# GpSimd put into written order as well, with a pair's values, turns, low parts and reciprocals written at earlier places

## The chip, the cores and the metric

One core of a Trainium2 chip runs the whole program. The time is device microseconds of that core, from runs of the same program; a profiled execution has a time of its own beside its span. The engines that matter are TensorE (PE: matmuls and transposes, into PSUM), VectorE (DVE), ScalarE (ACT), GpSimd (POOL) and SyncE (SP, which issues most transfers).

## The reference

```python
# 1. attention, 8 batches x 8 heads, 576 tokens, head size 64
scores = q @ k.T / 8                       # block mask: block(i) >= block(j), blocks of 64
attn   = exp(scores - max) ; attn /= sum + 1e-9
x      = (attn @ v) with heads side by side          # 8 x 576 x 512
# 2. token mixing of rank 32, then an MLP 512 -> 2048 -> 512
u = x + (x.T @ U @ V).T
y = u + relu(u @ w_ch1) @ w_ch2
# 3. gate: depthwise causal convolution over 5 tokens
out = (sigmoid(conv(y)) * (y @ w_val)) @ w_out
```

## The kernel before

**Tiles.** The 4608 tokens are cut into nine groups of 512. The MLP of a group runs in 16 steps of 128 hidden columns. A step's `emit_h1` is 12 matmuls into one PSUM bank (names `h`, three products for each of four pieces, since the float32 numbers are split into a high and a low part); ACT then makes the high part `hh` (L1167) and DVE the low part `hl` (L1168). `emit_o` is 12 matmuls that add the step before into four banks `acc`. Attention goes by pairs of heads: 32 pairs p, two heads a and b each. The stretch that the change touches is the one in which the MLP of groups 1 to 6 runs together with the attention of pairs 10 to 31.

**Order.** The MLP's matmuls are the ground, and after each half of `emit_h1` and of `emit_o` there is a gap, in which `gap` lets pieces of attention in. A pair takes `PERIOD` = 16 gaps. `events(p)` is the written table: each line gives the gap at which a piece is let in, whether it is one that PE takes part in (at most one of those in a gap), and the piece. Within an offset the pieces come in the order of the lines. Three pairs are under way at a time: p (scores, maxima, exponentials), q = p - 1 (values, normalising, transposing) and r = p - 2 (token mixing). PE's instructions always stand as the program writes them; from group 1 to group 6 those of DVE and ACT do as well (`manual_schedule`), while the order of POOL's is left to the scheduler. An offset only settles a place in each engine's queue: an engine starts no instruction before the one ahead of it.

**The pieces that matter here.**
- `scores(p, 0)` and `scores(p, 2)`: two halves of the score matmuls (L416), each half four PSUM banks; ACT copies every bank out (L421).
- `maxima(n)`, `max_c(n)`: a head's row maxima on DVE (L614, L633, L635, L636; then L647 to L657 and the transpose L660). `soften_sub(n)`: five subtractions on DVE (L667). `soften_exp(n)`: two exponentials on ACT (L683), then `emit_sum_a`, four additions on POOL (L690, L692). `emit_sum_b`: two reductions on DVE (L699).
- `values(q)`: the products with v (L733, L743), two banks `pPV`, copied out by ACT (L745).
- `pv_norm(q)`: three DVE instructions (L715, the reciprocal L716, the transpose L718) and one POOL multiplication of 128x576 (L719), which finishes the tile `xt`.
- `turn_all(q)`: transposes of `xt` on PE (L822, L824), two banks `pT`, and their high parts on ACT; `turn_lo(q)`: their low parts on DVE (L101, `x<-pT,x`).
- `g_product`, `g_sum`, `g_split`, `h_begin`, `h_end`: token mixing of pair r (names `pG`, `pH`, `ul`).

All of `h`, `pS`, `pPV`, `pT`, `pG` and `pH` share four PSUM banks in this stretch (`ps_p`); which bank a tile gets is settled when the program is built, and its first matmul waits for whoever read that bank last.

Of the kernel before, what the change touches and what calls it, by code (L numbers as in the profile page):

```python
# [22 lines left out]
def attn_moe_gate_kernel(ctx: ExitStack, tc: tile.TileContext, q, k, v, U, V, w1, w2, wval, convw, wout, out):  # L23
    nc = tc.nc
    B, H, S, D = q.shape
# [8 lines left out]
    NP = H // 2  # L34
# [54 lines left out]
    def f32(ap):  # L89
        return ap if ap.dtype == F32 else ap.bitcast(F32)  # L90
# [3 lines left out]
    def hi_act(o, i):  # L94
        act.copy(o, i)  # L95
# [4 lines left out]
    def lo(eng, o, i, h):  # L100
        eng.tensor_tensor(o, i, f32(h), op=ALU.subtract)  # L101
# [142 lines left out]
    def rot(tag, bufs=2, dtype=F32, n=S):  # L244
        return rot_p.tile([P, n], dtype, tag=tag, bufs=bufs, name=tag)
# [425 lines left out]
    def ev(n, j, a=0):  # L671
        return est[n][half_of[j]][:, soff[j] + a:soff[j] + wid[j]]
# [22 lines left out]
    def emit_sum_b(n):  # L695
        m = sums[n]
        r = tiny_p.tile([P, NB32], F32, tag="rs", bufs=3, name="rs")
        for o, t in ((slice(0, P // BL), ev(n, 0)[:, 0:P]), (slice(P // BL, NB32), m)):
            vec.tensor_reduce(r[:, o], t.rearrange("p (b a) -> p b a", a=BL), axis=AX.X, op=ALU.add, apply_transpose=True)  # L699
        sums[n] = r  # L700
# [12 lines left out]
    def pv_norm(pn, xt, f):  # L713
        r = tiny_p.tile([P, NB32], F32, tag="r0", name="r0")
        vec.tensor_scalar(r, f, 1e-9, None, op0=ALU.add)  # L715
        vec.reciprocal(r, r)  # L716
        rb = rot("t")
        vec.transpose(rb.rearrange("p (j a) -> p j a", a=32), r.rearrange("p (j o) -> p j o", o=1).to_broadcast([P, NB32, 32]))  # L718
        pool.tensor_tensor(xt, xt, rb, op=ALU.mult)  # L719
# [34 lines left out]
    normed = {}  # L754
# [57 lines left out]
    def turn_all(pn):  # L812
        xt = xts[pn]
        full = S // P
        if not xfix:
            xfix.append(rot("x", 1, F32R, NTT * 2 * P).rearrange("p (i c m) -> p i c m", c=2, m=P))
            pool.memset(f32(xfix[0][tok[-1][1]:, NTT - 1]), 0.0)
        x = xfix[0]
        gst[pn] = x
        ps = [ps_p.tile([P, 512], F32, tag="a", name="pT") for _ in range(2)]  # L820
        for i in range(full):
            pe.transpose(ps[0][:, i * P:(i + 1) * P], xt[:, i * P:(i + 1) * P], ident)  # L822
        t0, n = tok[full]
        pe.transpose(ps[1][:n, 0:P], xt[:, t0:t0 + n], ident)  # L824
        pairs = [(x[:, 0:full], ps[0][:, 0:full * P].rearrange("p (i m) -> p i m", m=P)), (x[:n, full:full + 1], ps[1][:n, 0:P].rearrange("p (i m) -> p i m", m=P))]
        for t, pv in pairs:
            hi_act(t[:, :, 0, :], pv)
        open_t[pn] = pairs

    def turn_lo(pn):  # L830
        for t, pv in open_t.pop(pn):
            lo(vec, t[:, :, 1, :], pv, t[:, :, 0, :])

    def g_product(pn):
        x = gst[pn].rearrange("p i c m -> p i (c m)")
        ps = ps_p.tile([P, 512], F32, tag="a", name="pG")
        for i in range(NTT):
            pe.matmul(ps[:, 0:2 * P], ust1[:, i, :], x[:, i, :], start=(i == 0), stop=(i == NTT - 1))
        open_t[pn] = ps

    def g_sum(pn):
        ps = open_t.pop(pn)
        g32 = rot("t")[:, 0:P]
        act.copy(g32, ps[:, 0:P])
        vec.tensor_tensor(g32, ps[:, P:2 * P], g32, op=ALU.add)
        open_t[pn] = g32

    def g_split(pn):
        g32 = open_t.pop(pn)
        g = rot("g", 4, F32R, P)  # L850
        hi_act(g, g32)
        lo(vec, g[2 * R:3 * R], g32[2 * R:3 * R], g[2 * R:3 * R])
        gst[pn] = g
# [68 lines left out]
    def soften_sub(n):  # L922
        emit_sub(n, 0)
        emit_sub(n, 1)

    def soften_exp(n):
        emit_exp(n)
        emit_sum_a(n)

    def max_c(n):  # L930
        for _ in emit_max_c(n):
            pass

    def maxima(n):
        emit_max_a(n)
        emit_max_b(n)

    def h_begin(pn, i):
        if i >= len(mix_pieces(pn // NP)):
            return  # L940
        if held(pn, i):
            later.append((pn, i))
        else:
            h_product(pn, i)

    def h_end(pn, i):
        if (pn, i) in open_h:
            h_sum(pn, i)
        if i and pn % NP == NP - 1:
            ready.add(pn // NP)  # L950
# [5 lines left out]
    def values(p):  # L956
        emit_pv(p, 0)
        emit_pv(p, 1)

    def events(p):  # L960

        a, b = 2 * p, 2 * p + 1
        new, q, r = a < NH, p - 1, p - 2
        first_ = p == PAIR0
        if new:
            yield 0, 1, lambda: scores(p, 0)
            yield 0, 0, lambda: (load_v(a), load_v(b))
        if first_:
            yield 2, 1, lambda: turn_all(r)
            yield 3, 0, lambda: turn_lo(r)  # L970
            yield 4, 1, lambda: g_product(r)
        else:
            yield 2, 1, lambda: g_product(r)
            yield 3, 0, lambda: g_sum(r)
            if q < B * NP:
                yield 3, 0, lambda: soften_exp(2 * q + 1)
            yield 4, 0, lambda: g_split(r)
        if new:
            yield 4, 1, lambda: scores(p, 2)
            yield 5, 0, lambda: (emit_corners(a), emit_corners(b), prep_t(p + 1))  # L980
        if first_:
            yield 6, 0, lambda: g_sum(r)
            yield 7, 0, lambda: g_split(r)
            yield 8, 1, lambda: h_begin(r, 0)
        else:
            yield 6, 1, lambda: h_begin(r, 0)
            if q < B * NP:
                yield 7, 0, lambda: emit_sum_b(2 * q + 1)
            yield 7, 0, lambda: h_end(r, 0)
            yield 7, 1, lambda: h_begin(r, 1)  # L990
            yield 8, 0, lambda: h_end(r, 1)
        if new:
            yield 8, 0, lambda: maxima(a)
        if q < B * NP:
            yield 9, 1, lambda: values(q)
        if new:
            yield 9, 0, lambda: max_c(a)
            yield 10, 0, lambda: soften_sub(a)
        if first_:
            yield 10, 0, lambda: h_end(r, 0)  # L1000
            yield 10, 1, lambda: h_begin(r, 1)
            yield 11, 0, lambda: h_end(r, 1)
        if q < B * NP:
            yield 12, 0, lambda: pv_norm(q, *normed.pop(q))
        if new:
            yield 12, 0, lambda: maxima(b)
            yield 12, 0, lambda: soften_exp(a)
        if q < B * NP:
            yield 14, 1, lambda: turn_all(q)
        if new:  # L1010
            yield 15, 0, lambda: max_c(b)
        if q < B * NP:
            yield 16, 0, lambda: turn_lo(q)
        if new:
            yield 16, 0, lambda: (emit_sum_b(a), soften_sub(b))

    def pair_tick(p):
        for off, pe_step, what in events(p):
# [361 lines left out]
    ordered = ExitStack()  # L1380
    for s in range(NS + LAG):
        g, f = divmod(s, NF)
        if g == 0:
            if convs:
                conv(2 * LEAD if f == 0 else 2)
                if not convs:
                    open_late()
        if f == 0 and g < B:
            while g == 1 and not pace[2] or g > 1 and g not in ready:
                pace[0] = 1.0  # L1390
                gap(FLUSH)
            if g == 1:
                at_gap["first"] = at_gap["count"]
                ordered.enter_context(tc.manual_schedule(engines={mybir.EngineType.DVE, mybir.EngineType.Activation}))
            if g == NG - 2:
                ordered.close()
            if g > 0:
                emit_o(s - LAG, gap)
            if pace[2] != 2:
                pace[2] = 0  # L1400
            aim(g)
        if s < NS:
            if g == NG - 1:
                if f == 2:
                    load_y(0)
                    split_tiles(0, pbp["y1"])
                if f == 5:
                    load_y(1)
            if cwt:
                wait_conv[0] -= 1  # L1410
                if not wait_conv[0]:
                    turn_conv()
            emit_h1(s, gap)
            load_w2(s)
            if g == NG - 1 and 4 <= f < 4 + 2 * ND:
                g_, d = divmod(f - 4, ND)
                if g_ == 0:
                    split_y(0, d)
                emit_gate(g_, d)
        if s >= LAG and not (f == 0 and g < B):  # L1420
            emit_o(s - LAG, gap)
# [54 lines left out]
```

## Time and profile before

| what | value |
|---|---|
| three runs | 1432.68, 1435.64, 1436.21 us; median 1435.64 |
| the profiled execution | 1434.67 us, span 1432.9 us, mean granted TensorE clock 0.993 |
| busy share of the span | PE 94%, weight loads 72%, DVE 68%, ACT 38%, POOL 31% |
| matmuls | 6840 |
| the chain that ended last | PE 60%, DVE 21%, ACT 6%, DMA 6%, POOL 3%, issue 3% |

A busy share is an average over stages. In a timeline row the first number is the start from the span's start, the second the length from the first to the last of the row's instructions; matmuls overlap, so the pace of PE is read from start to start. A number in brackets is idle time of the engine ahead of the row and who ended it.

### The profile page before, as it was taken

What the parts mean: (1) busy time and instruction counts of PE and PEld (TensorE: products, weight loads), DVE (VectorE), ACT (ScalarE), POOL (GpSimd) and SP (SyncE); (2) the same over time, 40 slices, a digit from 0 to 9 for tenths busy, and PEclk for the clock granted to TensorE, in tenths of its full rate; (3) what the DMA queues carried; (4) which work ended last, traced back from release to release, by engine and by line L of the source; (5) the groups of instructions that cost most, each with busy time, mean ns of one, the idle gap of its engine ahead of it and who ended that gap; (6) DMA issues with size and microseconds to landing.
All of it is one profiled execution on the core that took longest, in us unless ns stands there. A gap on an engine that the chain in (4) does not pass through costs nothing.

```text
span 1432.9 us, 20123 instructions
## 1 busy us (share of the span) xinstructions
PE 1343.8 (94%) x6840; PEld 1030.3 (72%) x6840; DVE 981.3 (68%) x2085; ACT 550.5 (38%) x1210; POOL 443.0 (31%) x648
## 2 busy tenths in 40 slices
PE   7888888999999999999999999999989999999999
PEld 4666665777777767776776777677768888788887
DVE  5986789577777677667677777776325145499991
ACT  5775544333343343344333433433223211444342
POOL 3353343322333242224223323422142100444210
PEclk9999999999999999999999999999999999999999
DMA  6677876534453353336344633522265443322311
GB/s 109 161 182 204 241 242 165 124 91 114 113 121 104 89 133 88 103 88 135 95 102 114 142 88 100 130 80 75 75 184 184 123 128 132 74 89 97 110 52 66
DMA packets 257936, 173.60 MB, mean 121 GB/s; under 512 B 202149, under 2 KB 222885, under 8 KB 257834
## 3 DMA queue, kind: packets, MB, share of 16 engines
q1 hardware_dynamic: 250282, 162.58, 40.3%
q0 software_dynamic: 5184, 9.44, 4.6%
q8 instruction: 54, 0.88, 0.3%
q10 hardware_dynamic: 2368, 0.30, 0.2%
q14 instruction: 48, 0.39, 0.1%
HBM read 135.57 MB, written 36.70 MB: 120 GB/s over the span
## 4 chain that ended last, share of the span: by engine, by line
PE 60%; DVE 21%; ACT 6%; DMA 6%; POOL 3%; issue 3%; SPq 1%; ACTq 0%; POOLq 0%; DVEq 0%
PE h L1139 18%; PE acc L1188 17%; PE o L1302 7%; PE val L1278 7%; PE pS L416 6%; DMA raw<-in_moe_w_ch_dram 3%; DVE rb L614 3%; DVE s L667 2%; POOL xt L719 2%; DVE hl L1168 2%; ACT e L683 1%; DVE rb L633 1%; POOL m L690 1%; PE pPV L733 1%; DVE mb L660 1%
## 5 line engine op out<-in xcount | busy, mean ns | idle before, releaser
L1188 PE MATMUL acc<-hh,w 128*128 128x512 f32 x1152 | 400.4, 401 | 2.1 <-ACT hh L1167 2.1
L1168 DVE SCALAR_TENSOR_TENSOR hl<-h,hh 128x512 fp32r<-128x512 f32 x144 | 98.7, 689 | 281.1 <-ACT hh L1167 280.3
L1188 PEld LDWEIGHTS acc<-hh,w 128*128 128x128 f32 x1152 | 218.9, 190 | 70.6 <-issue 22.5
L1188 PE MATMUL acc<-hl,w 128*128 128x512 f32 x576 | 228.2, 396 | 8.5 <-DVE hl L1168 8.5
L1139 PE MATMUL h<-uh,w1hi 128*128 128x512 f32 x576 | 232.8, 404 | 2.5 <-DVE hl L1168 1.5
L1139 PE MATMUL h<-uh,w1lo 128*128 128x512 f32 x576 | 225.7, 392 | 0.0
L1139 PE MATMUL h<-ul,w1hi 128*128 128x512 f32 x576 | 225.3, 391 | 0.0
L1167 ACT ACTIVATE hh<-h 128x512 fp32r<-128x512 f32 x144 | 85.7, 597 | 357.3 <-PE h L1139 353.8
L1188 PEld LDWEIGHTS acc<-hl,w 128*128 128x128 f32 x576 | 109.6, 190 | 32.2 <-DVE hl L1168 11.3
L1139 PEld LDWEIGHTS h<-uh,w1hi 128*128 128x128 f32 x576 | 108.5, 188 | 26.9 <-DVE hl L1168 1.9
L1139 PEld LDWEIGHTS h<-uh,w1lo 128*128 128x128 f32 x576 | 108.4, 188 | 23.4
L1139 PEld LDWEIGHTS h<-ul,w1hi 128*128 128x128 f32 x576 | 108.5, 188 | 19.6 <-issue 0.4
L416 PE MATMUL pS<-tq,tk 64*128 64x320 f32 (+4 forms) x576 | 103.4, 424 | 17.1 <-ACT s L421 12.6
L1260 DVE SCALAR_TENSOR_TENSOR gt<-yb,cw,gt 128x516 f32<-128x516 f32 (+1 forms) x144 | 115.3, 831 | 1.4
L101 POOL TENSOR_TENSOR yl<-yb,yh 128x512 fp32r<-128x512 f32 (+7 forms) x64 | 67.1, 1081 | 110.8 <-ACT yh L95 110.7
L416 PEld LDWEIGHTS pS<-tq,tk 64*128 64x128 f32 x576 | 54.0, 187 | 58.0 <-ACT s L421 22.8
L101 POOL TENSOR_TENSOR ul<-xt,uh 128x512 fp32r<-128x512 f32 (+7 forms) x64 | 53.0, 841 | 130.0 <-ACT uh L95 129.8
L421 ACT COPY s<-pS 128x320 f32<-128x320 f32 (+2 forms) x128 | 60.6, 505 | 45.7 <-PE pS L416 44.7
L733 PE MATMUL pPV<-e,vstk 128*64 128x192 f32 (+4 forms) x384 | 70.2, 336 | 0.0
L690 POOL TENSOR_TENSOR m<-e 128x448 f32<-128x448 f32 x24 | 29.5, 1230 | 127.8 <-ACT e L683 123.0
L667 DVE TENSOR_TENSOR s<-s,mb 128x64 f32<-128x64 f32 (+4 forms) x160 | 67.4, 484 | 0.5
L733 PEld LDWEIGHTS pPV<-e,vstk 128*64 128x64 f32 x384 | 46.8, 137 | 23.8 <-issue 16.0
(188 smaller groups left out, 2481.1 us busy)
## 6 DMA issues: line engine op xcount, KB each, us to landing
w<-w_s SPq DMA_DIRECT2D x144, 512.0 KB, 3.4
rawq<-in_q_dram SPq DMA_DIRECT2D x128, 72.0 KB, 2.6
out_dram<-ot SPq DMA_DIRECT2D x35, 256.0 KB, 2.0
rawk<-in_k_dram SPq DMA_DIRECT2D x124, 72.0 KB, 2.6
vstk<-in_v_dram SPq DMA_DIRECT2D x68, 128.0 KB, 3.3
raw<-in_moe_w_ch_dram SPq DMA_DIRECT2D x64, 128.0 KB, 2.4
raw<-in_moe_w_ch_dram SPq DMA_DIRECT2D x16, 512.0 KB, 4.3
w_s<-wo SPq DMA_DIRECT2D x16, 512.0 KB, 4.5
```

The lines of the kernel that those rows point to most:

```text
L101: eng.tensor_tensor(o, i, f32(h), op=ALU.subtract)
L416: pe.matmul(t[:, o:o + w], tk[me, kslice(j)], tq[me, a0:a1], start=True, stop=True)
L421: act.copy(stt[n][half_of[j]][:, d:d + o], t[:, 0:o])
L667: noted(3, vec.tensor_tensor(sv(n, j), sv(n, j), mb[:, q0[j]:], op=ALU.subtract))
L733: pe.matmul(ps[me, a0 - c0:c1 - c0], vpart(n)[:, j, :], est[n][half_of[j]][:, soff[j] + a0 - q0[j]:soff[j] + c1 - q0[j]], start=j == 0, st ...
L1139: pe.matmul(ps[:, 0:n], w[:, d, fs], x[:, d, 0:n], start=(d == 0 and i == 0), stop=(d == ND - 1 and i == 2))
L1167: act.activation(hh[:, 0:n], ps[:, 0:n], AF.Relu)
L1168: latest[0] = vec.scalar_tensor_tensor(hl[:, 0:n], ps[:, 0:n], 0.0, f32(hh[:, 0:n]), op0=ALU.max, op1=ALU.subtract)
L1188: pe.matmul(acc[d][:, 0:n], w[:, wi, ds], x[:, 0:n], start=(f == 0 and i == 0), stop=(f == NF - 1 and i == 2))
L1260: vec.scalar_tensor_tensor(gt[d][:, 0:gw], y[:, d, j:j + gw], cw[:, d, j:j + 1], gt[d][:, 0:gw], op0=ALU.mult, op1=ALU.add)
L1278: pe.matmul(ps[:, 0:n], w[:, d, es], x[:, d, 0:n], start=(i == 0), stop=(i == 3 * ND - 1))
L1302: pe.matmul(ps[:m, cs], x[:, e, a:a + m], w[:, e, cs], start=(i == 0), stop=(i == 3 * ND - 1))
```

## The change

The table `events` is rewritten, and POOL joins the engines that follow the written order.

```diff
         if first_:
-            yield 2, 1, lambda: turn_all(r)
-            yield 3, 0, lambda: turn_lo(r)
-            yield 4, 1, lambda: g_product(r)
+            yield 1, 1, lambda: turn_all(r)
+            yield 2, 0, lambda: turn_lo(r)
+            yield 3, 1, lambda: g_product(r)
...
             yield 8, 0, lambda: h_end(r, 1)
+        if q < B * NP:
+            yield 8, 1, lambda: values(q)
         if new:
-            yield 8, 0, lambda: maxima(a)
+            yield 8, 0, lambda: (maxima(a), max_c(a))
+        if first_:
+            yield 9, 1, lambda: h_begin(r, 0)
         if q < B * NP:
-            yield 9, 1, lambda: values(q)
+            yield 10, 0, lambda: pv_norm(q, *normed.pop(q))
         if new:
-            yield 9, 0, lambda: max_c(a)
             yield 10, 0, lambda: soften_sub(a)
...
+        if new:
+            yield 12, 0, lambda: (soften_exp(a), maxima(b))
         if q < B * NP:
-            yield 12, 0, lambda: pv_norm(q, *normed.pop(q))
+            yield 13, 1, lambda: turn_all(q)
+            yield 14, 0, lambda: turn_lo(q)
         if new:
-            yield 12, 0, lambda: maxima(b)
-            yield 12, 0, lambda: soften_exp(a)
-        if q < B * NP:
-            yield 14, 1, lambda: turn_all(q)
-        if new:
-            yield 15, 0, lambda: max_c(b)
-        if q < B * NP:
-            yield 16, 0, lambda: turn_lo(q)
-        if new:
-            yield 16, 0, lambda: (emit_sum_b(a), soften_sub(b))
+            yield 15, 0, lambda: (max_c(b), emit_sum_b(a), soften_sub(b))
...
-                ordered.enter_context(tc.manual_schedule(engines={mybir.EngineType.DVE, mybir.EngineType.Activation}))
+                ordered.enter_context(tc.manual_schedule(engines={mybir.EngineType.DVE, mybir.EngineType.Activation, mybir.EngineType.Pool}))
```

The number of instructions is the same on every engine, and outside this stretch their order is the same. In the changed file the lines behind the table have numbers lower by four (L1139 becomes L1135, L1168 becomes L1164, L1188 becomes L1184).

**First place, DVE, between the maxima of a pair's first head and those of its second.** `mb` is the spread maximum, `s` the scores, `hl` the MLP's low part; L715, L716 and L718 are `pv_norm`. Before:

```order
L660 STREAM_TRANSPOSE mb<-r_6858 128x576 [waits DVE_49]
L667 TENSOR_TENSOR s_6709<-s_6709,mb 128x64 [waits DVE_49]
L667 TENSOR_TENSOR s_6709<-s_6709,mb 128x192
L667 TENSOR_TENSOR s_6709<-s_6709,mb 128x576
L667 TENSOR_TENSOR s_6710<-s_6710,mb 128x448
L667 TENSOR_TENSOR s_6710<-s_6710,mb 128x320
L1168 SCALAR_TENSOR_TENSOR hl<-h_6902,hh 128x512 [waits Activation_49]
L715 TENSOR_SCALAR r_6932<-pPV 128x18 [waits PE_49]
L716 RECIPROCAL r_6932<-r_6932 128x18 [waits DVE_49]
L718 STREAM_TRANSPOSE t<-r_6932 128x576 [waits DVE_49]
L614 TENSOR_REDUCE rb<-s_6711 128x26
```

The same place in the changed kernel:

```order
L660 STREAM_TRANSPOSE mb<-r_6881 128x576 [waits DVE_49]
L715 TENSOR_SCALAR r_6909<-pPV 128x18 [waits Activation_49]
L716 RECIPROCAL r_6909<-r_6909 128x18 [waits DVE_49]
L718 STREAM_TRANSPOSE t<-r_6909 128x576 [waits DVE_49]
L667 TENSOR_TENSOR s_6709<-s_6709,mb 128x64
L667 TENSOR_TENSOR s_6709<-s_6709,mb 128x192
L667 TENSOR_TENSOR s_6709<-s_6709,mb 128x576
L667 TENSOR_TENSOR s_6710<-s_6710,mb 128x448
L667 TENSOR_TENSOR s_6710<-s_6710,mb 128x320
L1164 SCALAR_TENSOR_TENSOR hl<-h_6902,hh 128x512 [waits Activation_49]
L614 TENSOR_REDUCE rb<-s_6711 128x26 [waits Pool_49]
```

The three instructions of `pv_norm` have moved from behind the subtractions and `hl` to ahead of them.

**Second place, POOL, about the multiplication L719 that ends `pv_norm`.** L690 and L692 are the additions of `emit_sum_a`, L598 and L599 fill the masked corners of the scores. Before:

```order
L101 TENSOR_TENSOR ul<-xt,uh 128x192 [waits Activation_49]
L690 TENSOR_TENSOR m<-e 128x448 [waits Activation_49,Pool_49]
L719 TENSOR_TENSOR xt<-xt,t 128x576 [waits DMAHW6_49,DVE_49]
L692 TENSOR_TENSOR m<-m,e 128x320 [waits Pool_49]
L692 TENSOR_TENSOR m<-m,e 128x192 [waits Pool_49]
L692 TENSOR_TENSOR m<-m,e 128x64 [waits Pool_49]
L598 MEMSET za 64x2x64 [waits Activation_49,Pool_49]
```

The same place in the changed kernel:

```order
L101 TENSOR_TENSOR ul<-xt,uh 128x192 [waits Activation_49,Pool_49]
L719 TENSOR_TENSOR xt<-xt,t 128x576 [waits DMAHW1_49,DVE_49,Activation_49]
L690 TENSOR_TENSOR m<-e 128x448 [waits Activation_49]
L692 TENSOR_TENSOR m<-m,e 128x320 [waits Pool_49]
L692 TENSOR_TENSOR m<-m,e 128x192 [waits Pool_49]
L692 TENSOR_TENSOR m<-m,e 128x64 [waits Pool_49]
L690 TENSOR_TENSOR m<-s_6711,s_6712 128x448 [waits Activation_49,Pool_49]
```

L719 now stands ahead of the additions, where it stood behind the first of them, and the corners stand behind the second head's additions.

**Third place, PE, the first half of a pair's scores, in the middle of an `emit_o`.** `acc` is the MLP's sum; the rows of L416 are two banks of three widths, then two banks of width 320. Before:

```order
L1188 MATMUL acc_6690<-hh,w_7536 128x512
L416 MATMUL pS<-tq,tk 128x64 [waits DVE_49] x2
L416 MATMUL pS<-tq,tk 128x192 x2
L416 MATMUL pS<-tq,tk 128x256 x2
L416 MATMUL pS<-tq,tk 128x320 [waits Activation_49] x2
L1188 MATMUL acc_6691<-hh,w_7536 128x512
```

The same place in the changed kernel:

```order
L1184 MATMUL acc_6700<-hh,w_7542 128x512
L416 MATMUL pS<-tq,tk 128x64
L416 MATMUL pS<-tq,tk 128x64 [waits DVE_49]
L416 MATMUL pS<-tq,tk 128x192 x2
L416 MATMUL pS<-tq,tk 128x256 x2
L416 MATMUL pS<-tq,tk 128x320 [waits DVE_49] x2
L1184 MATMUL acc_6701<-hh,w_7542 128x512
```

The banks of width 320 waited for ACT and now wait for DVE. Counted along the programs, ACT's instructions there were the copies of the first two banks of the same scores. DVE's are now the second low part of `turn_lo` and the `hl` behind it, and the first low part is what the second row of width 64 waits for.

## Rows read from the trace of the kernel before

**Rows 1.** Busy time by windows, the sum line over 300 to 1000 us.
```profile
sum 700.00, PE 662.34 PEld 499.24 DVE 502.69 ACT 255.59 POOL 224.40; mean PE 94.62 PEld 71.32 DVE 71.81 ACT 36.51 POOL 32.06
```
**Rows 2.** Waits of PE, 290 to 1010 us: total us, times, longest.
```profile
PE pT L822 <- POOL xt L719: 15.1, 18, 1.1
PE pS L416 <- ACT s L421: 8.3, 14, 0.7
...
PE pS L416 <- ACT za L421: 4.2, 7, 0.7
```
**Rows 3.** Timeline of PE about one `turn_all`: start, length, instruction, idle before.
```profile
331.26 0.39 PE L1139 MATMUL h<-uh,w1lo 128*128 128x512 f32 x1
332.50 0.66 PE L822 MATMUL pT<-ident,xt 128*128 128x128 f32 x4 [0.85 <-POOL xt L719]
...
333.02 0.48 PE L1139 MATMUL h<-uh,w1hi 128*128 128x512 f32 x1
```
**Rows 4.** Timeline of PE, the first half of a pair's scores.
```profile
335.95 1.43 PE L416 MATMUL pS<-tq,tk 64*128 64x64 f32 x12
337.93 1.29 PE L416 MATMUL pS<-tq,tk 64*128 64x320 f32 x4 [0.55 <-ACT s L421]
339.15 0.50 PE L1188 MATMUL acc<-hh,w 128*128 128x512 f32 x1
```
**Rows 5.** Timeline of ACT, the first copy of those scores.
```profile
337.29 0.58 ACT L421 COPY s<-pS 128x512 f32<-128x512 f32 x1 [1.93 <-PE pS L416]
```
**Rows 6.** Timeline of PE, the second half of the same pair's scores.
```profile
345.43 1.56 PE L416 MATMUL pS<-tq,tk 64*128 64x448 f32 x8
346.92 0.50 PE L1188 MATMUL acc<-hh,w 128*128 128x512 f32 x1
```
**Rows 7.** Timeline of PE, values, then `emit_h1`, `emit_o` and the next `emit_h1`.
```profile
321.61 0.38 PE L733 MATMUL pPV<-e,vstk 128*64 128x192 f32 x1
...
324.55 0.50 PE L1139 MATMUL h<-uh,w1hi 128*128 128x512 f32 x1
...
330.13 0.39 PE L1139 MATMUL h<-uh,w1hi 128*128 128x512 f32 x1
```
**Rows 8.** Timeline of DVE from the first head's subtractions to the second's maxima.
```profile
326.19 1.16 DVE L667 TENSOR_TENSOR za<-za,mb 128x64 f32<-128x64 f32 x3
...
328.30 0.69 DVE L1168 SCALAR_TENSOR_TENSOR hl<-h,hh 128x512 fp32r<-128x512 f32 x1
328.90 0.17 DVE L715 TENSOR_SCALAR r<-pPV 128x18 f32<-128x18 f32 x1
...
330.11 1.86 DVE L614 TRANSPOSE_TENSOR_REDUCE rb<-s 128x26 f32<-128x832 f32 x2
332.00 1.30 DVE L633 TENSOR_TENSOR rb<-rb 128x10 f32<-128x10 f32 x3
...
333.43 0.57 DVE L636 COPY r<-rb 128x4 f32<-128x4 f32 x1
```
**Rows 9.** Timeline of POOL in the same stretch.
```profile
329.93 1.15 POOL L690 TENSOR_TENSOR m<-e 128x448 f32<-128x448 f32 x1 [6.67 <-ACT e L683]
331.04 1.41 POOL L719 TENSOR_TENSOR xt<-xt,t 128x576 f32<-128x576 f32 x1
332.40 1.97 POOL L692 TENSOR_TENSOR m<-m,e 128x320 f32<-128x320 f32 x3
```
**Rows 10.** Timeline of DVE: L633 with POOL idle, and beside POOL at 397.68 us.
```profile
323.41 0.44 DVE L633 TENSOR_TENSOR rb<-rb 128x10 f32<-128x10 f32 x3
...
397.68 2.87 DVE L633 TENSOR_TENSOR rb<-rb 128x10 f32<-128x10 f32 x3
```
**Rows 11.** Timeline of ACT, the second exponential of the first head.
```profile
328.95 0.83 ACT L683 ACTIVATE e<-zb 128x768 f32<-128x768 f32 x1
```
**Rows 12.** Groups of DVE by form, 290 to 1010 us: `turn_lo`; busy us, mean ns.
```profile
L101 DVE TENSOR_TENSOR x<-pT,x 128x512 fp32r<-128x512 f32 x22 | 14.4, 652 | 0.0
...
L101 DVE TENSOR_TENSOR x<-pT,x 64x128 fp32r<-64x128 f32 x22 | 5.9, 266 | 0.0
```

More of the change, by code (lines that the diff above doesn't have):

```diff
@@ L981, in events @@
         if first_:
-            yield 6, 0, lambda: g_sum(r)
-            yield 7, 0, lambda: g_split(r)
-            yield 8, 1, lambda: h_begin(r, 0)
+            yield 5, 0, lambda: g_sum(r)
+            yield 6, 0, lambda: g_split(r)
         else:
```

## The prediction

> **What bounds the kernel now.** The windows come first: between 300 and 1000 us PE is busy 662 of 700 us and DVE 503, ACT 256, POOL 224 [rows 1], so PE sets the pace there and 38 us of it are idle. The list of waits then says for whom PE stops: 18 times for POOL's multiplication L719 before a pair's transposes, 15.1 us, and 21 times for ACT's copies in the first half of a pair's scores, 12.5 us [rows 2]. What a stop costs is read from starts in the timeline, since a matmul's record outlasts its pace. That pace is (330.13 - 324.55) / 24 = 0.23 us [rows 7].
>
> - Transposes: the last matmul ahead starts at 331.26, the first transpose at 332.50 [rows 3]. 1.24 - 0.23 = 1.01 us are lost where the row shows 0.85 idle. For the 18 waits: 15.1 + 18 x 0.16 = 18.0 us.
> - First half of the scores: 339.15 - 335.95 = 3.20 us [rows 4]. The second half, with no such wait, takes 346.92 - 345.43 = 1.49 us for 448 + 320 columns a head [rows 6]. The first has 64 + 192 + 256 + 320 = 832, so it should take 1.49 x 832 / 768 = 1.61. The loss is 1.59 us a pair, three times the 0.55 that the row names: the wait for the copies [rows 5] comes on top of two banks that do not run side by side. For 21 pairs 33.4 us.
>
> Together 51.4 us hang on these two stops, and the change touches both. It adds and removes no instruction; all its costs are places in queues.
>
> **Values and transposes earlier.** Values move from the end to the middle of an `emit_o`, by six matmuls, 1.4 us; they then run from about 320.2 to 323.2 (their length is 324.55 - 321.61 = 2.94) [rows 7]. PE's own order loses nothing by it. The transposes move ahead of an `emit_h1`, and PE comes to them at 330.13 [rows 7]. None of the pieces moved in the ordinary pair issues a transfer, so SP's queue is passed by nothing.
>
> **Reciprocals ahead of the subtractions, L719 first on POOL.** DVE is through with the first head's maxima at 326.19 [rows 8], three us after the values end. `pv_norm` now starts there instead of at 328.90, and takes DVE 330.11 - 328.90 = 1.21 us [rows 8]. L719 can start at about 327.5: POOL is idle for 6.67 us before 329.93 [rows 9] and nothing is ahead of L719 any more. It takes 1.41 us [rows 9], and ends between 328.9 and 329.4. PE wants it at 330.13, so some 0.8 us are in hand. The 18.0 us come back. Without that cover each 0.1 us of lateness costs 0.1 us a pair.
>
> **What it collides with.** The subtractions start 1.21 us later, at 327.40, and L719 now runs beside them; before, POOL was idle while they ran [rows 8, 9]. DVE's instructions with two SBUF inputs suffer beside POOL: the three of L633 take 0.44 us alone, 1.30 beside L719 and L692, and 2.87 in the worst place shown [rows 10, 8, 9]. No row here shows subtractions beside L719, so the delay lies between 0 and L719's 1.41. I take 1.2: L719 asks during the second subtraction, and the third must wait for most of it, which is what L633 does beside L719. The Trainium skill, "SBUF — State Buffer", section "SBUF: two separate sides", speaks against this part of the change: GpSimd and a DVE instruction with two SBUF inputs take one port pair as an exclusive lock, and the one that comes second is blocked for the whole instruction. By that rule the delay would be the whole 1.41 and the sum below about 3 us smaller; rows 10 agree in kind.
>
> The subtractions took 328.30 - 326.19 = 2.11 [rows 8], so they end at 327.40 + 2.11 + 1.2 = 330.7 instead of 328.3. Behind them on DVE stand `hl` (0.60 to the next start) and the second head's maxima: L614 from 331.3 to 333.2 (1.89), then L633 to L636, which took 334.0 - 332.00 = 2.0 beside POOL [rows 8]. What POOL does beside them now: the second exponential starts at 330.7 and takes 0.83 [rows 11], L690 follows at 331.7 (1.11 to the next), the three L692 end at 334.8 (1.97) [rows 9]. So they still meet POOL, but for its shorter additions. Bounds are about 0.7 and 3.6 us (2.0 and the 1.57 by which 2.87 exceeds 1.30); I take 1.5, nearer to the ordinary row. The maxima end at 334.7. `hl` itself is not wanted until the second matmul of an `emit_o` after 333.4, so no one waits for it.
>
> **Low parts two gaps earlier.** `turn_lo` now stands ahead of the pair's last `hl` and of `max_c(b)`, so the two `pT` banks are free in time to serve the next scores, and the banks of width 320 no longer wait for the copies of the first two. In their place PE waits for DVE: the first low part (0.65) ends at 335.35, the second (0.27) at 335.6 [rows 12], the `hl` behind at 336.3. PE: transposes 333.02 - 332.50 = 0.52 [rows 3], twelve matmuls 2.8, half an `emit_o` 1.4, a switch 0.1: from 330.13 the scores are reached at 334.9. It waits some 0.5 us for the first low part; the other two are there when wanted. The half then costs 1.61 + 0.5 = 2.1 instead of 3.2: 1.1 us gained in each ordinary pair.
>
> Of the 21 pairs, five stand at the change from one group to the next. There the `hl` that the `emit_o` ahead of the scores needs is on DVE ahead of the low parts; these follow within 0.92 us, while PE does 1.4 us of `emit_o`. So no wait remains and the whole 1.59 is gained. The 2.87 us of L633 at 397.68 lie at such a place [rows 10]; whether they shrink I leave out.
>
> **The rest.** The corners now follow the second head's additions on POOL, and the first head's maxima wait for them; but ahead of those maxima DVE has a reduction of those same additions, so only the fills themselves count, and POOL is idle 6.67 us in that stretch [rows 9]. Nothing, or up to 1 us a pair (21 us) if the cover were gone. The first pair of the stretch has a table of its own; between a gain and a loss of 2 us, taken as nothing.
>
> **The sum.** 18.0 + 16 x 1.1 + 5 x 1.59 = 43.6 us. From the profiled execution's own 1434.7 us (span 1432.9) that gives 1391; the median of the runs shown is 1.0 above that execution, so 1392.
>
> **The rivals.**
> 1. *The low parts are in time everywhere* (the lock costs less than 0.7 us). For it: POOL needs only one turn. Gain 18.0 + 33.4 = 51.4, 1384.
> 2. *L719 gets no turn before all five subtractions are over*, at 329.5. It ends at 330.9 and PE waits 0.9 for it as before; but then DVE is not delayed, the low parts are in time: 18 x 0.1 + 33.4 = 35, 1401. Against it: POOL's row of L719 and DVE's of L633 interleave [rows 8, 9].
> 3. *The wait for copies turns wholly into one for the low parts*: they end a further 1.1 us later, at 336.4, as when L633 to L636 take 2.6. Gain 18.0 + 8.0 = 26, 1410.
> 4. *Slower: DVE falls behind.* If the low parts end 2.1 us later than I have them (337.4), an ordinary pair gains nothing. The port decides: if the subtractions lose 1.57 us, as L633 does at 397.68, and L633 again 1.57 to 2.9 [rows 10], the low parts come about 3.3 us late, each of 21 pairs is 3.3 later than the sum has it, and 43.6 - 69 is a loss of 26: 1461. Against it: L633's long row is at a group change, where POOL also issues four transfers, and DVE has 28% idle to recover [rows 1].
> 5. *It moves nothing*: what PE no longer waits for, it waits for in another place of the same pair, 1435. Against it: the waits removed have two different releasers.
>
> **How the numbers follow.** Forecast 0.47, rival 1 0.15, 2 0.12, 3 0.16, 4 0.05, 5 0.05. A difference of 0.3% (4 us) is about what runs of this kernel can tell from none. Faster by more 0.90, within 0.05, slower 0.05. The range 1380 to 1414 takes in the forecast and rivals 1 to 3 with a few us beside them; the chance outside is that of 4 and 5 and of a miss in the estimates.
>
> **What would show it.** In the profile after: no wait of PE for L719; the first half of the scores at 1.6 to 2.2 us, its wait now put down to DVE's low parts; a subtraction lengthened by about 1.2 us beside L719; a pair every 30.4 us instead of 32.5; PE busy 97% or more between 300 and 960 us. Wrong would be: transposes still waiting for L719 (rival 2), scores of 3 us behind L101 (rival 3), or PE idle before `emit_o` for `hl` (rival 4).

## The result, and the profile after

The changed kernel takes 1391.4 us (median of 4 runs, 1389.8 to 1395.5) beside 1434.2 us of the kernel before on the same chip: a ratio of 0.9705, 95% interval 0.9679 to 0.9731. The profiled execution took 1395.5 us, with a span of 1393.7, so it is the longest of the four; the others had spans of 1388.0 to 1389.6. Why, the second profile of the same kernel shows below.

The waits of PE in the ordered stretch, 290 to 1010 us (engine, waiting line, releaser: us in total, times, longest), beside [rows 2]:

```profile
PE acc L1184 <- DVE hl L1164: 7.8, 5, 2.7
PE pH L884 <- DVE hl L1164: 6.9, 6, 1.3
PE h L1135 <- DVE hl L1164: 1.5, 1, 1.5
PE pS L416 <- DVE x L101: 0.5, 1, 0.5
```

The two releasers on which the prediction rests, L719 and ACT's copies L421, are gone. What is left is `hl`. The busy time by windows says the same: 645.67 of 660 us, 97.8%.

```profile
300.00:960.00 660.00, 645.67 (x3538) 497.44 (x3537) 515.03 (x1202) 250.89 (x524) 227.75 (x380) 0.99 0.45 111
```

One ordinary pair in the timeline (start, length, instruction), DVE, then POOL, then PE; they answer to [rows 8], [rows 9] and [rows 3, 4]:

```profile
325.26 2.35 DVE L667 TENSOR_TENSOR za<-za,mb 128x64 f32<-128x64 f32 x3
...
331.01 1.33 DVE L633 TENSOR_TENSOR rb<-rb 128x10 f32<-128x10 f32 x3
...
332.67 0.87 DVE L101 TENSOR_TENSOR x<-pT,x 128x512 fp32r<-128x512 f32 x2
...
325.47 1.53 POOL L719 TENSOR_TENSOR xt<-xt,t 128x576 f32<-128x576 f32 x1 [4.15 <-issue]
329.52 1.16 POOL L690 TENSOR_TENSOR m<-e 128x448 f32<-128x448 f32 x1 [2.51 <-ACT e L683]
...
328.13 0.60 PE L822 MATMUL pT<-ident,xt 128*128 128x128 f32 x4
...
328.60 0.48 PE L1135 MATMUL h<-uh,w1hi 128*128 128x512 f32 x1
...
332.88 2.30 PE L416 MATMUL pS<-tq,tk 64*128 64x64 f32 x16
335.12 0.50 PE L1184 MATMUL acc<-hh,w 128*128 128x512 f32 x1
...
358.61 0.60 PE L822 MATMUL pT<-ident,xt 128*128 128x128 f32 x4
```

L719 ends at 327.0, and PE comes to the transposes at 328.13 without a stop. Beside it the first three subtractions take 2.35 us where they took 1.16. The low parts start at 332.67, some 0.2 us before PE reaches the scores, and the half takes 335.12 - 332.88 = 2.24 us instead of 3.20. The list of waits shows nothing for it, but it is 0.5 longer than the 1.72 that the half takes where the low parts are early (below). The next pair's transposes come 30.48 us later.

At a change of group (DVE, then PE) the picture is another:

```profile
387.28 3.29 DVE L667 TENSOR_TENSOR s<-s,mb 128x64 f32<-128x64 f32 x5
390.50 1.89 DVE L614 TRANSPOSE_TENSOR_REDUCE rb<-s 128x26 f32<-128x832 f32 x2
392.42 1.53 DVE L633 TENSOR_TENSOR rb<-rb 128x10 f32<-128x10 f32 x3
...
394.72 0.68 DVE L1164 SCALAR_TENSOR_TENSOR hl<-h,hh 128x512 fp32r<-128x512 f32 x1
...
394.40 0.39 PE L1184 MATMUL acc<-hh,w 128*128 128x512 f32 x1
395.45 0.50 PE L1184 MATMUL acc<-hl,w 128*128 128x512 f32 x1 [0.66 <-DVE hl L1164]
```

The `hl` of the new group's first `emit_h1` stands behind the second head's maxima, and PE's second matmul of `emit_o` waits for it. By starts the five changes lose 0.92, 1.13, 1.76, 2.40 and 3.99 us there, 10.2 in all, about 1.1 of the last in a slower clock (below); before they lost some 1.22 each, 6.1. The kernel before in the list of waits, and one row of POOL at the last change:

```profile
PE acc L1188 <- DVE hl L1168: 4.8, 5, 1.0
```

```profile
886.03 1.16 POOL L101 TENSOR_TENSOR ul<-xt,uh 128x448 fp32r<-128x448 f32 x1 [3.79 <-ACT uh L95]
```

The loss grows from change to change. A `ul` stands there on POOL just ahead of L719, and it widens from 192 columns at the first change to 448 at the last. From the start of the subtractions to the next instruction of DVE it is 3.22 us at the first change and 3.84 at the last, where it was 2.02 before. At the last change the subtractions also start 1.1 us later than at the first, measured against the `emit_o` that waits.

### The profile page after: what moved, and what is told of

It is laid out like the page before. It is cut to its first block, busy times and chain, and to the rows that moved or that the text cites. A ratio compares the mean times of both kernels' runs of the same rounds, so it can differ in the third digit from the quotient of the medians.

```text
span 1393.7 us, 20067 instructions
## 1 busy us (share of the span) xinstructions
PE 1329.7 (95%) x6840; PEld 1032.1 (74%) x6840; DVE 994.5 (71%) x2085; ACT 547.2 (39%) x1210; POOL 445.8 (32%) x648
## 4 chain that ended last, share of the span: by engine, by line
PE 71%; DVE 17%; DMA 5%; ACT 4%; issue 2%; SPq 1%; POOL 0%; ACTq 0%; DVEq 0%
PE acc L1184 23%; PE h L1135 21%; PE o L1298 7%; PE val L1274 7%; PE pS L416 6%; PE pPV L733 3%; DMA raw<-in_moe_w_ch_dram 3%; DVE rb L614 2%; DVE s L667 2%; PE pS L455 1%; DVE rb L633 1%; DVE hl L1164 1%; PE pG L838 1%; PE pPV L543 1%; DVE xt L896 1%
## 5 line engine op out<-in xcount | busy, mean ns | idle before, releaser
L1184 PE MATMUL acc<-hh,w 128*128 128x512 f32 x1152 | 407.8, 405 | 2.5 <-ACT hh L1163 2.5
L1184 PEld LDWEIGHTS acc<-hh,w 128*128 128x128 f32 x1152 | 220.1, 191 | 72.0 <-issue 23.2
L1164 DVE SCALAR_TENSOR_TENSOR hl<-h,hh 128x512 fp32r<-128x512 f32 x144 | 98.5, 685 | 223.5 <-ACT hh L1163 223.4
L1184 PE MATMUL acc<-hl,w 128*128 128x512 f32 x576 | 229.4, 398 | 11.5 <-DVE hl L1164 11.5
L1135 PE MATMUL h<-uh,w1hi 128*128 128x512 f32 x576 | 230.8, 401 | 2.5 <-DVE hl L1164 1.5
L1135 PE MATMUL h<-uh,w1lo 128*128 128x512 f32 x576 | 225.2, 391 | 0.0
L1135 PE MATMUL h<-ul,w1hi 128*128 128x512 f32 x576 | 224.7, 390 | 0.0
L1184 PEld LDWEIGHTS acc<-hl,w 128*128 128x128 f32 x576 | 110.3, 191 | 34.4 <-DVE hl L1164 14.2
L1135 PEld LDWEIGHTS h<-uh,w1hi 128*128 128x128 f32 x576 | 108.4, 188 | 26.5 <-DVE hl L1164 1.9
L1135 PEld LDWEIGHTS h<-uh,w1lo 128*128 128x128 f32 x576 | 108.2, 188 | 23.6
L1135 PEld LDWEIGHTS h<-ul,w1hi 128*128 128x128 f32 x576 | 108.5, 188 | 20.1 <-issue 0.4
L101 POOL TENSOR_TENSOR yl<-yb,yh 128x512 fp32r<-128x512 f32 (+7 forms) x64 | 67.1, 1082 | 111.2 <-ACT yh L95 111.0
L416 PE MATMUL pS<-tq,tk 64*128 64x320 f32 (+4 forms) x576 | 91.5, 422 | 5.5 <-ACT s L421 4.5
L667 DVE TENSOR_TENSOR s<-s,mb 128x64 f32<-128x64 f32 (+4 forms) x160 | 86.1, 602 | 0.0
L416 PEld LDWEIGHTS pS<-tq,tk 64*128 64x128 f32 x576 | 52.2, 190 | 36.3 <-issue 21.5
L421 ACT COPY s<-pS 128x320 f32<-128x320 f32 (+2 forms) x128 | 59.6, 510 | 41.0 <-PE pS L416 40.9
L690 POOL TENSOR_TENSOR m<-s,s 128x448 f32<-128x448 f32 x16 | 18.3, 1144 | 151.2 <-ACT s L683 150.9
L719 POOL TENSOR_TENSOR xt<-xt,t 128x576 f32<-128x576 f32 x24 | 36.3, 1511 | 91.5 <-DVE t L718 55.4
```

The source lines that it names most:

```text
L416: pe.matmul(t[:, o:o + w], tk[me, kslice(j)], tq[me, a0:a1], start=True, stop=True)
L421: act.copy(stt[n][half_of[j]][:, d:d + o], t[:, 0:o])
L667: noted(3, vec.tensor_tensor(sv(n, j), sv(n, j), mb[:, q0[j]:], op=ALU.subtract))
L1135: pe.matmul(ps[:, 0:n], w[:, d, fs], x[:, d, 0:n], start=(d == 0 and i == 0), stop=(d == ND - 1 and i == 2))
L1164: latest[0] = vec.scalar_tensor_tensor(hl[:, 0:n], ps[:, 0:n], 0.0, f32(hh[:, 0:n]), op0=ALU.max, op1=ALU.subtract)
L1184: pe.matmul(acc[d][:, 0:n], w[:, wi, ds], x[:, 0:n], start=(f == 0 and i == 0), stop=(f == NF - 1 and i == 2))
```

## The experiments

Every kernel was timed beside the kernel before on its own chip; ratios carry their 95% intervals. Names of lines shift by one to eight lines between them.

**Low parts late.** The low parts go back behind the last maxima.

```diff
-            yield 14, 0, lambda: turn_lo(q)
-        if new:
-            yield 15, 0, lambda: (max_c(b), emit_sum_b(a), soften_sub(b))
+            pass
+        if new:
+            yield 15, 0, lambda: max_c(b)
+        if q < B * NP:
+            yield 16, 0, lambda: turn_lo(q)
+        if new:
+            yield 16, 0, lambda: (emit_sum_b(a), soften_sub(b))
```

> The changed kernel with one part undone: the low parts of a pair's turns stand behind the second head's last maxima (max_c) again, two gaps later. Theory (the low parts free the two transpose banks that the width-320 scores use): the first half of a pair's scores goes back to about 3.2 us behind ACT's copies, from 2.0 to 2.2 in the 16 ordinary pairs and 1.7 in four of the five at a group change. 16 x 1.1 + 4 x 1.5 = 23.6 us are lost, 1415 us; the transposes still do not wait for L719. Rival (the scores gained because the transposes or the reciprocals came earlier, and the low parts' place is indifferent): the half stays near 2 us, 1391.

1422.0 us, ratio 0.9904 (0.9885 to 0.9923). PE's waits:

```profile
PE acc L1188 <- DVE hl L1168: 7.8, 5, 2.6
PE pS L416 <- ACT s L421: 7.1, 14, 0.7
...
PE pS L416 <- ACT za L421: 3.6, 7, 0.7
```

The wait for ACT's copies is back in all 21 pairs, and the half takes 3.14 to 3.81 us, at the last change 4.81. So the low parts' place is what rid the scores of the copies, as in the prediction. Of the 28.3 us between this profiled span and the changed kernel's (1422.0 and 1393.7) the halves account for 26.7; 2.1 were there at the first scores of the stretch. The 23.6 expected were too few because the early pairs, and the last change (in a slower clock), came out longer than before.

**Reciprocals late.** The reciprocals and L719 go back behind the first head's subtractions; all else as changed.

```diff
-            yield 10, 0, lambda: pv_norm(q, *normed.pop(q))
+            pass
         if new:
             yield 10, 0, lambda: soften_sub(a)
+        if q < B * NP:
+            yield 10, 0, lambda: pv_norm(q, *normed.pop(q))
```

> The changed kernel with one part undone: the reciprocals and the multiplication L719 are written behind the first head's five subtractions again. Theory: the subtractions lose their 1.24 us of delay, but L719 then starts some 2.1 us after its start in the changed kernel plus that, at about 328.5 on its clock, and ends near 329.9, where PE comes to the transposes at 328.1: about 1.8 us of wait in each of 16 ordinary pairs, 29 us, while the low parts are in time and the scores give back 0.5 in each, 8 us. 1391 + 21 = 1412, with the wait put to L719. Rival (the collision costs more than the earlier start is worth): 1391 or less.

1393.4 us, ratio 0.9713 (0.9698 to 0.9727), which can't be told from the changed kernel. Waits of PE, and DVE's and PE's timeline:

```profile
PE pT L822 <- POOL xt L719: 13.6, 20, 1.7
```

```profile
320.08 1.16 DVE L667 TENSOR_TENSOR za<-za,mb 128x64 f32<-128x64 f32 x3
...
329.80 1.79 PE L416 MATMUL pS<-tq,tk 64*128 64x64 f32 x16
331.51 0.50 PE L1186 MATMUL acc<-hh,w 128*128 128x512 f32 x1
```

My 1.8 us a pair was wrongly added: without the delay of 1.24 the subtractions themselves end earlier, and L719 starts 2.1 us later, not 3. The stop before the transposes is 0.6 to 1.0 us. What matters is the other side. With no POOL work beside the subtractions (1.16 us again) the half of the scores takes 1.72 us in all 21 pairs, and no `emit_o` waits for `hl`. The earlier reciprocals thus buy some 17 us at the transposes, by starts, and pay about as much: 7.6 us at the scores (the changed kernel's 21 halves take 43.7 us together, 21 x 1.72 are 36.1) and 10.2 us in the waits for `hl` at the changes.

**L719 on VectorE.**

```diff
-        pool.tensor_tensor(xt, xt, rb, op=ALU.mult)
+        vec.tensor_tensor(xt, xt, rb, op=ALU.mult)
```

> The changed kernel with the multiplication L719 issued on VectorE instead of GpSimd, in the same written place, right behind the transpose of the reciprocals. Theory (L719 on GpSimd delays the subtraction beside it by its own length): VectorE takes about 0.75 us for it, as for a subtraction of the same 576 columns, and no subtraction is longer than 0.75 any more, so VectorE is 0.5 us a pair earlier, not later. The first half of the scores loses its remaining 0.3 to 0.6 us: 16 x 0.45 = 7 us, and the wait for hl at the five group changes gets 0.5 shorter, 2.5 us: 1382. Rival (the long subtraction is no delay by GpSimd but the time of the work itself): VectorE has 0.75 us more in each pair, the low parts come later by it, 16 x 0.75 = 12 us lost, 1403.

1381.05 us, ratio 0.9624 (0.9609 to 0.9638), as expected in all. The 21 halves of scores take 36.7 us together, 7.0 less, as forecast; the waits for `hl` at the changes lose 3.5 us by starts, 6.7 less, where 2.5 were forecast. Subtractions in the changed kernel, then here (ns min/median/max):

```profile
L667 DVE TENSOR_TENSOR s<-s,mb x150: 180/483/1990, 293.0 to 965.1; 128x64 f32<-128x64 f32 x30, 128x192 f32<-128x192 f32 x30, 128x576 f32<-128x576 f32 x30, 128x448 f32<-128x448 f32 x30
```

```profile
L667 DVE TENSOR_TENSOR s<-s,mb x150: 180/482/754, 293.1 to 950.0; 128x64 f32<-128x64 f32 x30, 128x192 f32<-128x192 f32 x30, 128x576 f32<-128x576 f32 x30, 128x448 f32<-128x448 f32 x30
...
L719 DVE TENSOR_TENSOR xt<-xt,t x23: 757/758/1211, 292.5 to 961.9; 128x576 f32<-128x576 f32 x23
```

A subtraction that took up to 1.99 us takes at most 0.75 once L719 no longer runs beside it on GpSimd: 1.24 us of it were the neighbour's. VectorE does the multiplication in 0.76 us, so handing it to GpSimd costs VectorE 0.5 us more than doing it. The rule cited in the prediction from the Trainium skill, "SBUF — State Buffer", section "SBUF: two separate sides", by which the one that comes second waits until the first is through, would make it 1.41 only if both asked at once. In the ordinary pair above the long subtraction starts at 325.26 + 2.35 - 1.99 = 325.62, with 1.38 us of L719 still to run; the measured 1.24 stays 0.14 below that.

**Low parts first.** Of the second head's maxima the five small instructions follow the low parts.

```diff
-            yield 12, 0, lambda: (soften_exp(a), maxima(b))
+            yield 12, 0, lambda: (soften_exp(a), emit_max_a(b))
 ...
             yield 14, 0, lambda: turn_lo(q)
         if new:
+            yield 14, 0, lambda: emit_max_b(b)
```

> The changed kernel with the second head's maxima cut in two: the two reductions L614 stay where they are, the five small instructions L633 to L636 follow the low parts instead of standing ahead of them. Theory (what is left of PE's waits is the place of L633 to L636, 1.3 to 2.7 us long beside GpSimd's additions, ahead of the low parts and, at a group change, ahead of the hl that the next emit_o needs): the first half of the scores takes 1.65 to 1.75 us everywhere, 16 x 0.4 = 6.5 us and 1.6 at the last group change; at the five group changes the wait of emit_o for hl (10.5 us in all by starts) goes to under 1 us each. Together 15 to 18 us: 1375. Rival (VectorE as a whole is late in these places, and the order of a few small instructions only moves the wait): within 3 us of 1391.

1377.2 us, ratio 0.9600 (0.9585 to 0.9614). DVE in an ordinary pair, and at the first change of group:

```profile
328.27 0.84 DVE L101 TENSOR_TENSOR x<-pT,x 128x512 fp32r<-128x512 f32 x2
329.04 0.86 DVE L633 TENSOR_TENSOR rb<-rb 128x10 f32<-128x10 f32 x3
...
388.70 0.65 DVE L1165 SCALAR_TENSOR_TENSOR hl<-h,hh 128x512 fp32r<-128x512 f32 x1
389.27 0.86 DVE L101 TENSOR_TENSOR x<-pT,x 128x512 fp32r<-128x512 f32 x2
390.07 1.00 DVE L633 TENSOR_TENSOR rb<-rb 128x10 f32<-128x10 f32 x3
```

The half of the scores takes 1.72 us in 18 of 21 pairs, and of the 10.2 us at the changes 0.2 are left. So the place of L633 to L636 alone can take away the last waits, with no less work for VectorE; taking work from VectorE (the run before) takes away a part of them too.

**Reciprocals alone.** The kernel before, with `pv_norm` written ahead of `soften_sub(a)` and GpSimd in written order.

```diff
             yield 9, 0, lambda: max_c(a)
+            pass
+        if q < B * NP:
+            yield 10, 0, lambda: pv_norm(q, *normed.pop(q))
+        if new:
             yield 10, 0, lambda: soften_sub(a)
...
         if q < B * NP:
-            yield 12, 0, lambda: pv_norm(q, *normed.pop(q))
+            pass
...
-                ordered.enter_context(tc.manual_schedule(engines={mybir.EngineType.DVE, mybir.EngineType.Activation}))
+                ordered.enter_context(tc.manual_schedule(engines={mybir.EngineType.DVE, mybir.EngineType.Activation, mybir.EngineType.Pool}))
```

> The kernel before with one part of the change alone: the reciprocals and L719 ahead of the first head's subtractions, and GpSimd in written order (so that L719 comes first there); values, turns and low parts stay where they were. Theory (each stop of PE has its own remedy): the transposes no longer wait for L719, 18 us come back; the first half of the scores stays at 3.2 us behind ACT's copies; the subtraction beside L719 is longer by 1.24 us, which at the five group changes makes emit_o wait longer for hl, 4 us in all: 1436 - 18 + 4 = 1422. Rival (the gain of the change is in the earlier values and transposes): within 5 us of 1436.

1425.3 us, ratio 0.9941 (0.9926 to 0.9956). PE's waits:

```profile
PE acc L1192 <- DVE hl L1172: 8.8, 5, 2.6
PE pS L416 <- ACT s L421: 7.1, 14, 0.7
```

No wait for L719 is left, the scores still wait for the copies, and the waits for `hl` at the changes have grown, from 4.8. So each of the two stops has its own remedy, but the gain is 8.6 us where 14 were forecast: the 21 halves of scores take 3.6 us more than before (70.7 instead of 67.1), a part of it in a slower clock behind the last change.

**GpSimd's order alone.** The kernel before with the last line of that diff only.

> The kernel before with GpSimd in written order and nothing else changed. Theory (GpSimd was idle ahead of L719 in ordinary pairs, so the order cannot bring it forward): 1434, within 4 us, with the transposes waiting about 1.0 us for L719 in 17 pairs as before. Rival (the order itself holds a part of the gain): 1425 or less, or, if the corners behind the additions hold up the maxima, 1440 or more.

1419.3 us, ratio 0.9891 (0.9873 to 0.9908): the theory fell. The timeline of GpSimd and PE, and PE's waits:

```profile
328.50 1.43 POOL L719 TENSOR_TENSOR xt<-xt,t 128x576 f32<-128x576 f32 x1 [7.00 <-ACT e L683]
329.89 1.14 POOL L690 TENSOR_TENSOR m<-e 128x448 f32<-128x448 f32 x1
...
329.45 0.39 PE L1139 MATMUL h<-uh,w1lo 128*128 128x512 f32 x1
329.98 0.66 PE L822 MATMUL pT<-ident,xt 128*128 128x128 f32 x4
```

```profile
PE pT L822 <- POOL xt L719: 2.0, 11, 0.5
```

My expectation overlooked what [rows 9] show: the addition L690 stood ahead of L719. With the written order it stands behind. L719 then starts 0.95 us before the last matmul ahead of the transposes, where it was 0.22 [rows 3, 9], and the stop shrinks from 1.01 us to 329.98 - 329.45 - 0.23 = 0.30. Summed over the 18 stops, by starts, that gives back 12.1 of the 18.0 us, with no collision. Adding the earlier reciprocals to it (the run before) made the kernel slower by 6 us. About 4 of these lie in TensorE's clock: behind the last change, where PE waits 2.63 us for `hl`, the granted clock of the run with the reciprocals fell (its window from 920 to 930 us; behind the counts: granted clock, DMA share, GB/s).

```profile
920.00:930.00 10.00, 8.16 (x27) 5.44 (x28) 6.98 (x20) 1.92 (x4) 1.32 (x3) 0.61 0.38 66
```

With GpSimd's order alone the wait there is 0.97 us and the clock of the same window 1.00. The mean clock of all four executions was 0.985 to 0.988 with the reciprocals, and 0.992 to 0.994 without.

**GpSimd free.** The changed kernel without that line.

> The changed kernel with GpSimd left to the scheduler's order again; the table stays. Theory (the written order on GpSimd gives nothing by itself: with the reciprocals written early the scheduler puts L719 and every low part ul in the same places, and only additions, corners and one transfer change theirs): within 4 us of 1391 to 1394. Rival (the written order keeps additions and corners out of the way of the maxima): slower by 5 us or more.

1396.3 us, ratio 0.9728 (0.9708 to 0.9748), against 0.9705 and 0.9719 of the changed kernel: the order's worth here is a few us at most, and the intervals overlap. With the reciprocals written early, L719 stands ahead of the first head's additions in the scheduler's order as well.

**Reciprocals late, low parts first.** The edits of both those runs together.

> The kernel in which the low parts stand ahead of L633 to L636, with the reciprocals and L719 behind the first head's subtractions. Theory (in the changed kernel the delay that L719 puts on a subtraction takes back nearly all that the earlier reciprocals give; where the low parts come ahead of L633 to L636 there is room for the delay, and the earlier reciprocals are worth their whole gain): the transposes wait 0.6 to 1.0 us in 20 pairs as in the run with the reciprocals alone late, 15 us, and the scores were in time already: 1377 + 14 = 1391. Rival (the earlier reciprocals are worth 2 us in either order): 1379.

1394.3 us, ratio 0.9730 (0.9714 to 0.9746). PE's waits:

```profile
PE pT L822 <- POOL xt L719: 14.4, 20, 1.7
```

Here the earlier reciprocals are worth 1394.3 - 1377.2 = 17 us (19 by the ratios), where with the low parts behind L633 to L636 they were worth 2, which the runs can't tell from nothing.

**Both.** Low parts first, and L719 on VectorE.

> The low parts ahead of L633 to L636 and L719 on VectorE, together. Theory: the two take the same waits of PE (the low parts at the scores, hl at a group change), so their 10 and 14 us do not add; what is left with the low parts first is 0.4 at the first scores, 1.5 at two others and 0.2 at a group change, some 2 us: 1375 us. Rival (they add, because VectorE's time is what the pairs are short of): 1391 - 24 = 1367.

1375.4 us, ratio 0.9590 (0.9576 to 0.9604); the gains don't add, since both take the same waits. It is the fastest version of the study, though its interval overlaps that of low parts first alone. Its 21 first halves of scores all take 1.72 us.

**The changed kernel again.**

> The changed kernel as it is, for a second profile. Theory: median 1391 again; the first profile's span is some 4 us above those of the other runs of the same kernel, and this excess lies in the long wait at the last group change (892 to 901 us, 6 us by starts), which a second profile shows shorter. Rival (the excess lies elsewhere, as in the part behind 1100 us): the same 6 us there.

1393.85 us, ratio 0.9719 (0.9700 to 0.9737). The profiled execution has a span of 1388.0. The last change of group in the first profile, PE's timeline and windows (behind the counts: granted clock, DMA share, GB/s):

```profile
892.47 0.39 PE L1184 MATMUL acc<-hh,w 128*128 128x512 f32 x1
895.52 0.79 PE L1184 MATMUL acc<-hl,w 128*128 128x512 f32 x1 [2.66 <-DVE hl L1164]
896.11 1.05 PE L1184 MATMUL acc<-hh,w 128*128 128x512 f32 x2
896.96 0.63 PE L1184 MATMUL acc<-hl,w 128*128 128x512 f32 x1
...
897.95 3.36 PE L416 MATMUL pS<-tq,tk 64*128 64x64 f32 x16
901.24 0.79 PE L1184 MATMUL acc<-hh,w 128*128 128x512 f32 x1
```

```profile
895.00:900.00 5.00, 4.48 (x17) 3.40 (x19) 4.76 (x16) 0.00 (x0) 0.24 (x1) 0.52 0.51 90
```

And in the second:

```profile
893.16 0.50 PE L1184 MATMUL acc<-hl,w 128*128 128x512 f32 x1 [2.67 <-DVE hl L1164]
893.50 0.63 PE L1184 MATMUL acc<-hh,w 128*128 128x512 f32 x2
893.97 0.39 PE L1184 MATMUL acc<-hl,w 128*128 128x512 f32 x1
```

```profile
895.00:900.00 5.00, 5.00 (x31) 3.98 (x30) 4.08 (x12) 1.74 (x4) 0.00 (x0) 1.00 0.32 86
```

The wait is the same, so that half of the theory fell. In the first profile the clock fell behind it (0.52 over the window, much of it at the lower level, 1.2 GHz): two matmuls take 0.85 us from start to start instead of 0.47, and the half of the scores 901.24 - 897.95 = 3.29 instead of 1.72. By starts this half `emit_o`, the scores and the next half take 1.1, 1.6 and 0.4 us more than in the second profile, 3.0 in all. There the clock stayed at 1.00. The other 2.4 us were there already at the first scores of the stretch (302.0 and 299.6 us).

## Why the prediction was right, and where it was not

The time, 1391.4, is the 1392 forecast, and the mechanism is the one forecast; that the two numbers are within 1 us is partly luck, since one term failed and others made up for it. The terms fared as follows.

- *Transposes.* No wait for L719 remains, so the 18.0 us came back, and the block of five is 0.06 shorter. But the prediction gave all of it to the earlier reciprocals and L719's place together; 12.1 us need only the place.
- *The collision.* Taken as 1.2 us, measured as 1.24.
- *L633 to L636.* Taken as 1.5 us, measured as 332.67 - 331.01 = 1.66.
- *Scores in the 16 ordinary pairs.* Taken as 2.1 us, measured as 2.10 on average (2.60 in the first, 1.87 in the last): the gain is 17.5 us, where 16 x 1.1 = 17.6 were forecast. Inside, two sizes were off and cancelled: the undisturbed half takes 1.72 us, not 1.61 scaled from the second half's columns, and the wait is 0.4, not 0.5.
- *The five changes of group.* This step failed: "So no wait remains and the whole 1.59 is gained." The low parts are in time there, and the half takes 1.72 us at four of the five. But I asked only whether PE would wait for the low parts, and not whether the `hl` ahead of them, for which PE waited already, would come later too. DVE's collision, 1.2 us at the first change and 1.8 at the last, and PE's earlier arrival fall on it. The scores gave 5.8 us (the last half lies in the slow clock), `hl` took 10.2 - 6.1 = 4.1 more, and 1.7 us are left of 8.0. In the second profile, without the slow clock, it is 7.4 - 3.1 = 4.3.
- *Corners.* In the changed kernel's trace DVE waits nowhere for POOL: nothing, as said.

These make 18.0 + 17.5 + 1.7 = 37.2, with the shorter transposes 38.5, of the 39.2 us between the two profiled spans. The medians lie 42.8 us apart; the profiled execution is the longest of its four. Against the second profile the terms make 41.2 of 44.9 us. The rest is in no term of the sum, and 2.8 us of it are there at the first scores of the stretch (303.48 and 299.64, less 1.0 at the transposes), though that start differs by 2.4 between two executions of the same kernel.

Rivals 1 and 3 put the half of the scores at 1.6 and 3.2 us; it lies between. In rival 2 L719 gets no turn beside the subtractions, and it got one in every pair. Rival 4, DVE falling behind, did come, but at the five changes of group instead of in 21 pairs, and for some 2 us each.

What the runs add is that the parts don't have separate worths. GpSimd's order alone gives 16 us; the earlier reciprocals cost 6 us on top of that order (some 4 of them by the clock), give next to nothing in the change as made, and 17 once the low parts stand ahead of L633 to L636. The earlier places of the values and of the transposes were undone in no run by themselves; what they are worth stays open.

## What to carry to other kernels

When a stop is removed by starting work earlier on a second engine, list every instruction on the first engine that then runs beside it, and follow that delay to each consumer that already waits, not only to the one that the edit is about. Work given to GpSimd that meets VectorE's two-input instructions can cost VectorE more than doing it itself (here 1.24 us against 0.76). Order a queue by who is waited for next: moving five small instructions behind the ones that PE needs gave 14 us more, at no cost.

## What the hardware showed unexpectedly

After the same wait of PE, 2.66 and 2.67 us, TensorE's granted clock fell in one execution of the changed kernel (0.52 in the window behind it) and stayed at 1.00 in another. With the low parts late it fell too, to 0.50, behind a wait of 2.64, and with the reciprocals alone, to 0.61, behind one of 2.63. With GpSimd left free it fell behind waits of 2.09 us (0.50 from 772 to 777 us) and 2.29 (0.66 from 900 to 905), while behind 2.12 to 2.27 us in four other profiles it stayed at 1.00. A single wait of 2.1 to 2.7 us can thus cost about twice itself, in some executions only; why in those stays open.

VectorE's copy L636, with a single input, is also longer beside GpSimd's additions: 0.30 us at 332.46 in the changed kernel beside L692, and 0.16 at 321.98 with GpSimd idle.

```profile
321.98 0.16 DVE L636 COPY r<-rb 128x4 f32<-128x4 f32 x1
...
332.46 0.30 DVE L636 COPY r<-rb 128x4 f32<-128x4 f32 x1
```
